# Clearing transfers placed behind the last weight load of a mixture kernel

## Chip, cores and metric

The kernel runs on one core of a Trainium2 chip. The metric is the device time of one execution in microseconds (us). The core has five engines with an instruction list each: TensorE (PE in the profile; PEld is its weight load), VectorE (DVE), ScalarE (ACT), GpSimd (POOL) and SyncE (SP). SP issues nearly all transfers here. Each engine goes through its list in order.

## What is computed

Three stages follow each other: attention with a window and a few sink positions, a gated MLP (called the first mixture here, `moe_`), and a routed mixture of eight experts (`moe2_`). Shapes: 2 x 8 heads x 768 positions x 64; then 1536 tokens of 512 values, an inner width of 1536, and eight experts with an inner width of 1024.

```python
scores = where(is_sink | in_window, q @ k.T / sqrt(D), -1e9)
x = softmax(scores) @ v                      # 1536 x 512 after the heads are joined
g = x @ w_gate                               # 512 x 1536
x = (g * sigmoid(g) * (x @ w_val)) @ w_out   # first mixture
do = x @ w_skip > 0                          # second mixture: only these tokens
e = argmax(x[do] @ gate); p = softmax(x[do] @ gate)[e]
out = x; out[do] += p * (relu(x[do] @ w1[e]) @ w2[e])
```

The arrays are float32, but the three weights of the first mixture arrive as 64-bit floats.

## The kernel before

The 1536 tokens are twelve blocks of 128. The first mixture runs in three phases of four blocks each (`PHASES`); a phase goes through twelve chunks of the inner width, and for each chunk PE makes the gate and value products (`proj`, L551) and, one chunk later, adds to the four output accumulators (`down`, L563). Attention of the next blocks is interleaved with that: while phase 0 works on blocks 0 to 3, PE also does blocks 4 to 7.

The weights of the first mixture come in 36 pieces of 512 KB (`load_w`, L154): gate, value and output for each of the twelve chunks. Since they are 64-bit, a piece lands in one of three staging buffers (`st`) and is converted to float32 by two steps on ACT (L169, L170) and two on DVE (L174, L175) in `convert`. The converted weights stay in fast memory for all phases, so the conversions may run well ahead of the chunk that needs them. `convert_w` converts one piece and starts the load of the piece three further on; `todo` holds the pieces whose load has not been traced yet. `prep` later splits a converted piece into a high and a low part (ring, L74 and L77) for PE.

For the experts, tokens are scattered into rows of a scratch tensor `xs` in DRAM, one region for each expert (L771, an indirect transfer issued on POOL). Rows that no token takes must hold zeros and a token number out of range, so the first 192 rows of each of the eight regions are written beforehand: `clear_rows` (L667) fills one tile `trash` with zeros on POOL and issues eight transfers of 387 KB from it on SP (L672), one at each `next(rows)` of the main loop. The main loop (L1373 to L1387) counts the steps `s` of phase 0, of which there are 37, three to a chunk; `clear_rows` starts at step 6, and the eight transfers are traced at the even steps from 14 to 28. `load_w` traces its last piece at step 29.

The order within an engine's list is set by a scheduler: it knows what each instruction depends on, and puts an instruction into its engine's list as soon as, by its own reckoning, the instruction could start and nothing traced earlier is ready. So work that is ready soon stands in the lists far ahead of the place where it was traced. `tc.issue_after(ins)` adds an edge of order: what is traced under it on the engine of `ins` comes behind `ins` in that engine's list, with no wait for `ins` to finish.

The q and k of the later blocks (from the ninth on) are loaded in 16 + 16 small pieces (`load_qk`, L109) and turned on DVE (`turned_a`, L322).

Of the kernel before, what the change touches and what calls it, by code (L numbers as in the profile page):

```python
# [10 lines left out]
I32 = mybir.dt.int32  # L11
# [4 lines left out]
P = 128  # L16

@with_exitstack
def build(ctx: ExitStack, tc: tile.TileContext, q, k, v, n_sink, window,
          wg, wv, wo, w_skip, w_gate, w1, w2, out):  # L20
    nc = tc.nc
# [30 lines left out]
    RW = DM + 4  # L52
    ES = NT + 2 * P
    HP = P // 2
# [75 lines left out]
        return rings[i // 4][:, i % 4, :]  # L130

    staged = []

    wsrc = {"g": wg, "v": wv, "o": wo}
    todo = [(nm, c) for c in range(NFC) for nm in "gvo"]

    def load_w():

        if not todo:
            return  # L140
        nm, c = todo.pop(0)
        src = wsrc[nm]
        t = wpc[nm, c // 4]
        if nm == "o":
            dst, s = t[:, c % 4, :], src[c * P:(c + 1) * P, :]
        else:
            dst = t[:, :, (c % 4) * P:(c % 4 + 1) * P]
            s = src[:, c * P:(c + 1) * P].rearrange("(a p) f -> p a f", p=P)
        if not wide:
            nc.sync.dma_start(out=dst, in_=s)  # L150
            return
        st = stp.tile([P, 512, 2], I32, tag="st", name="st")
        si = st if nm == "o" else st.rearrange("p (a f) t -> p a f t", a=KD)
        nc.sync.dma_start(out=si.rearrange("p f t -> p (f t)") if nm == "o" else si.rearrange("p a f t -> p a (f t)"), in_=s.bitcast(I32))  # L154
        staged.append((dst, si))

    def convert(dst, si):
# [21 lines left out]
    def convert_w():  # L179
        if staged:  # L180
            convert(*staged.pop(0))
        converted[0] += 1
        load_w()
# [438 lines left out]
    xs = dram.tile([NE * ES, RW], F32, name="xs")  # L622
# [11 lines left out]
    def make_trash(trash):  # L634
        nc.gpsimd.memset(trash, 0.0)
        nc.gpsimd.iota(trash.bitcast(I32)[:, DM + 1:DM + 2], pattern=[[0, 1]], base=NT, channel_multiplier=0)

    def make_routing_consts():
        with nc.allow_non_contiguous_dma(reason="small"):
            nc.sync.dma_start(out=wgs[:, :, 0:NE], in_=w_gate.rearrange("(a p) e -> p a e", p=P))  # L640
            nc.sync.dma_start(out=wgs[:, :, NE:NE + 1], in_=w_skip.rearrange("(a p o) -> p a o", p=P, o=1))
        nc.gpsimd.memset(ones, 1.0)
        act_copy(upper, ident[:, HP:P])
        nc.gpsimd.affine_select(out=before, in_=ones, compare_op=ALU.is_gt, fill=0.0, base=0, pattern=[[1, P]], channel_multiplier=-1)
        it = mo.tile([P, RW], F32, tag="x2", name="it", bufs=4)[:, 0:P].bitcast(I32)
        nc.gpsimd.iota(it, pattern=[[1, P]], base=0, channel_multiplier=0)
        nc.gpsimd.tensor_copy(slot, it)
        first_block = tc.issue_after(begun["DVE"])
        first_block.__enter__()

        nc.vector.tensor_scalar(out=code, in0=slot[:, 0:NE + 1], scalar1=float(NE), scalar2=-1.0, op0=ALU.subtract, op1=ALU.mult)

        nc.vector.tensor_scalar(out=first, in0=slot[:, 0:NE + 1], scalar1=float(ES // P), scalar2=None, op0=ALU.mult)
        nc.gpsimd.memset(first[:, NE:NE + 1], float(4 * NE * ES // P))
        nc.gpsimd.iota(tokid, pattern=[[P, NT // P]], base=0, channel_multiplier=1)
        nc.vector.tensor_copy(seen, first)
        first_block.__exit__(None, None, None)

    def turn_gates():
        t = attp.tile([P, KD, P], F32, tag="att", name="wgT")  # L660
        for kk in range(KD):
            nc.tensor.transpose(out=t[0:NE + 1, kk], in_=wgs[:, kk, :], identity=ident)
        c = mo.tile([P, RW], F32, tag="x2", name="wgc", bufs=4)[0:NE + 1, 0:DM]
        act_copy(c, t[0:NE + 1].rearrange("p a f -> p (a f)"))
        nc.sync.dma_start(out=wgt, in_=c)

    def clear_rows():  # L667

        trash = mo.tile([P, RW], F32, tag="x2", name="trash", bufs=4)
        make_trash(trash)  # L670
        for e in range(NE):
            nc.sync.dma_start(out=xs[e * ES:e * ES + P + HP, :].rearrange("(b p) c -> p b c", b=2),  # L672
                              in_=trash[0:(P + HP) // 2].unsqueeze(1).to_broadcast([(P + HP) // 2, 2, RW]))
            yield

    def route(pools, toks, rows, apart=None):
# [166 lines left out]
    def finish(g, tiles):  # L843
        take, turn, logits, close = routing(g, tiles)
        n = len(tiles)
        for i, t in enumerate(tiles):
            take(i, acc.pop((g, t)))
        for i in range(n):
            turn(i)
            if i > 0:  # L850
                logits(i - 1)
        logits(n - 1)
        close()
# [485 lines left out]
    load_v(0)  # L1339
    make_consts()  # L1340
    load_w()
    load_w()
    load_qk(1)
    load_w()
# [23 lines left out]
    for i, (g, t0, t1, c0, c1, want) in enumerate(PHASES):  # L1368
        pieces = (want - done) * (3 * NPAIR + 2)
        slots = 3 * (c1 - c0) - 1  # L1370
        s = 0
        emitted = 0
        for _ in mlp(i):  # L1373
            s += 1
            while done < want and emitted < pieces * s / slots:
                done = next(at, NB_ALL)
                emitted += 1
            if i == 0 and s == 6:
                make_routing_consts()
                rows = clear_rows()  # L1380
            if i == 0 and s > 12 and s % 2 == 0:
                next(rows, None)
            if i == 0 and s == 24:
                turn_gates()
            while apart and units < min(units_all, (s - 3) * units_all // 22):
                next(apart)
                units += 1  # L1387
        while done < want:
            done = next(at, NB_ALL)
        if i == 0:  # L1390
            for _ in rows:
                pass
        if done == NB_ALL and late is None:
            early.close()
            late = fast.enter_context(tc.tile_pool(name="late", bufs=2))
        if apart:
            for _ in apart:
                pass
            apart = None
        if i in APART:  # L1400
            apart = finish_apart(g, range(t0, t1), late_rows if late else early_rows)
            next(apart)
            units, units_all = 0, (t1 - t0) * (NE + 1) + 1
        elif i + 1 == len(PHASES):
            with tc.manual_schedule(engines={mybir.EngineType.PE}):
                finish_last(g, range(t0, t1), late)
                experts(late)
        elif c1 == NFC:
            finish(g, range(t0, t1))
# [33 lines left out]
```

## Time and profile before

| | us |
|---|---|
| median of three runs | 608.57 |
| lowest and highest run | 607.16, 608.84 |
| the profiled execution, its own time | 606.38 |
| span of its profile | 604.7 |

| engine | busy us in the span |
|---|---|
| PE | 569.9 |
| DVE | 456.1 |
| ACT | 347.8 |
| POOL | 206.7 |

Times in the profile count from the start of the span. A wait names the instruction that released it as the profile infers it. In an order of time, the bracket at the end of a row is the idle time of that engine just before, and what ended it.

### The profile page before, as it was taken

The page shows a single profiled execution, that of the slowest core. Times are in us where ns is not written, and L with a number is a line of the kernel's source. Part 1 is how long each engine was busy: PE and PEld are TensorE (multiplying, and loading weights), DVE is VectorE, ACT ScalarE, POOL GpSimd, SP SyncE. Part 2 cuts the span into 40 slices and gives each one's busy share as a digit, 9 for nine tenths or more (in the row PEclk, how much of TensorE's full clock was granted, in tenths as well). Part 3 has the DMA queues.
Part 4 walks back from the last instruction along what each step waited for, and adds up shares of the span by engine and source line. Part 5 has one row for each costly group of instructions (what it writes and reads, how often), then busy time and mean ns, then how long its engine had stood idle before and what let it go on. Part 6 is the DMA issues. An engine that isn't in the chain of part 4 may idle for free. (4 is left out here: it accounts for less than half of the span.)

```text
span 604.7 us, 10096 instructions
## 1 busy us (share of the span) xinstructions
PE 569.9 (94%) x3049; PEld 440.3 (73%) x3049; DVE 456.1 (75%) x1170; ACT 347.8 (58%) x818; POOL 206.7 (34%) x291
## 2 busy tenths in 40 slices
PE   7999999799999999999999999999987999999992
PEld 4657767567777777777888888888875877777771
DVE  4798897897656899986564999854368897999930
ACT  4898786776555565655444453443146666766710
POOL 3474362566444241412320100030143334536310
PEclk7899999999999999999999999999997999999997
DMA  8866888653302422000002531300159777879401
GB/s 200 195 167 159 244 247 260 190 175 88 88 11 36 111 59 68 19 19 0 19 1 88 192 105 53 123 30 1 63 169 325 256 259 244 286 252 315 171 5 35
DMA packets 90597, 80.53 MB, mean 133 GB/s; under 512 B 53515, under 2 KB 65803, under 8 KB 90530
## 3 DMA queue, kind: packets, MB, share of 16 engines
q1 hardware_dynamic: 87730, 74.07, 40.9%
q0 software_dynamic: 2512, 5.68, 2.7%
q8 instruction: 29, 0.48, 0.3%
q14 instruction: 38, 0.31, 0.2%
q10 hardware_dynamic: 288, 0.00, 0.0%
HBM read 70.09 MB, written 12.00 MB: 136 GB/s over the span
## 5 line engine op out<-in xcount | busy, mean ns | idle before, releaser
L551 PE MATMUL gv<-xt,ring 128*128 128x512 f32 x864 | 216.9, 401 | 0.0
L551 PEld LDWEIGHTS gv<-xt,ring 128*128 128x128 f32 x864 | 158.1, 188 | 38.3 <-issue 2.0
L74 ACT ACTIVATE ring<-w 128x512 fp32r<-128x512 f32 x113 | 70.8, 629 | 94.9 <-PE gv L551 72.4
L77 DVE TENSOR_TENSOR w<-stage,w 128x512 fp32r<-128x512 f32 x96 | 85.2, 930 | 8.1 <-ACT w L74 6.3
L563 PE MATMUL acc<-ring,hh 128*128 128x512 f32 x256 | 82.5, 403 | 0.0
L74 ACT ACTIVATE w<-stage 128x512 fp32r<-128x512 f32 x128 | 71.5, 628 | 14.6 <-DMA stage<-in_moe_w_dram 10.5
L77 POOL TENSOR_TENSOR w<-stage,w 128x512 fp32r<-128x512 f32 x32 | 45.8, 1433 | 94.7 <-DVE ring L77 59.4
L77 DVE TENSOR_TENSOR ring<-w,ring 128x512 fp32r<-128x512 f32 x77 | 54.0, 701 | 26.7 <-ACT ring L74 26.7
L77 POOL TENSOR_TENSOR ring<-w,ring 128x512 fp32r<-128x512 f32 x36 | 48.7, 1354 | 51.1 <-ACT ring L74 46.7
L563 PEld LDWEIGHTS acc<-ring,hh 128*128 128x128 f32 x256 | 46.4, 188 | 11.8 <-issue 1.2
L718 DVE CUSTOM_DVE_ANT_0 wl<-x,wl 128x512 f32<-128x512 f32 x72 | 50.2, 697 | 1.1
L563 PE MATMUL acc<-ring,hl 128*128 128x512 f32 x128 | 50.9, 398 | 0.0
L364 ACT ACTIVATE p<-p,st 128x132 f32<-128x132 f32 x96 | 38.2, 400 | 17.2 <-DVE st L360 16.4
L1076 PE MATMUL yps<-w,hT 128*128 128x512 f32 x192 | 46.8, 398 | 0.8 <-ACTq L1115 0.5
L397 POOL TENSOR_SCALAR_AFFINE_SELECT pt<-pt 128x256 f32<-128x256 f32 x40 | 21.9, 548 | 73.6 <-ACT pt L74 73.6
L1050 PE MATMUL hps<-w,xh 128*128 128x512 f32 x128 | 42.8, 416 | 1.0
L1076 PEld LDWEIGHTS yps<-w,hT 128*128 128x128 f32 x192 | 35.4, 188 | 9.8 <-ACTq L1115 1.3
L344 PE MATMUL s<-kq 64*128 64x260 f32 (+1 forms) x144 | 34.9, 418 | 3.1 <-DVE st L360 1.1
L594 DVE TENSOR_TENSOR th<-th,gv 128x512 f32<-128x512 f32 x36 | 24.5, 681 | 14.4 <-PE gv L551 14.3
L771 POOL DMA_INDIRECT xs<-x,pi x12 | 12.1, 1012 | 60.2 <-issue 35.0
L175 DVE SCALAR_TENSOR_TENSOR w<-w,st 128x512 int32<-128x512 int32 x36 | 30.2, 839 | 2.3 <-ACT w L170 1.0
L344 PEld LDWEIGHTS s<-kq 64*128 64x128 f32 x144 | 16.9, 196 | 20.5 <-issue 10.5
(199 smaller groups left out, 958.7 us busy)
## 6 DMA issues: line engine op xcount, KB each, us to landing
stage<-in_moe_w_dram SPq DMA_DIRECT2D x128, 256.0 KB, 4.5
st<-in_moe_w_gate_dram SPq DMA_DIRECT2D x12, 512.0 KB, 4.9
st<-in_moe_w_val_dram SPq DMA_DIRECT2D x12, 512.0 KB, 4.9
st<-in_moe_w_out_dram SPq DMA_DIRECT2D x12, 512.0 KB, 5.6
xs<-trash SPq DMA_DIRECT2D x8, 387.0 KB, 5.6
vb<-in_v_dram SPq DMA_DIRECT2D x12, 256.0 KB, 4.6
out_dram<-x SPq DMA_DIRECT2D x12, 256.0 KB, 3.1
wl<-wgt SPq DMA_DIRECT2D x10, 256.0 KB, 4.1
```

Source lines behind the costliest of these rows:

```text
L74: nc.scalar.activation(out=out, in_=in_, func=ACTF.Copy, scale=scale)
L77: return (eng or nc.vector).tensor_tensor(out=out, in0=in_, in1=hi.bitcast(F32), op=ALU.subtract).ins
L175: nc.vector.scalar_tensor_tensor(out=di, in0=di, scalar=3, in1=low, op0=ALU.logical_shift_left, op1=ALU.bitwise_or)
L344: m_ = nc.tensor.matmul(out=ss[h][:, 0:nk], lhsT=x_, rhs=y_, start=m == 0, stop=m == len(terms) - 1)
L364: nc.scalar.activation(out=p[:, h], in_=p[:, h], func=ACTF.Exp, scale=-1.0, bias=st[:, h:h + 1], accum_out=su[:, h:h + 1])
L397: nc.gpsimd.affine_select(out=d[:, 0], in_=d[:, 1], compare_op=ALU.is_ge, fill=0.0, base=0, pattern=[[0, 2], [1, P]], channel_multiplier=-1)
L551: nc.tensor.matmul(out=ps, lhsT=w_[:, kk * P:(kk + 1) * P], rhs=x_[:, kk, t0 * P:t1 * P], start=kk == 0 and m == 0, stop=kk == KD - 1 and ...
L563: nc.tensor.matmul(out=acc[g, t], lhsT=h_[:, s], rhs=w_, start=c == 0 and m == 0, stop=c == last and m == 2)
L594: nc.vector.tensor_tensor(out=th, in0=th, in1=vp, op=ALU.mult)
L718: nc.vector.tensor_tensor_reduce(out=junk, in0=x2s[t][:, 0:DM], in1=row, scale=1.0, scalar=0.0, op0=ALU.mult, op1=ALU.add, accum_out=lp[:, ...
L1050: nc.tensor.matmul(out=ps[half], lhsT=x_[:, kk, :], rhs=w_[:, kk, :], start=kk == 0 and m == 0, stop=kk == KD - 1 and m == 2)
L1076: nc.tensor.matmul(out=y, lhsT=h_[:, c, :], rhs=w_[:, c % 4, :], start=c == 0 and m == 0, stop=c == NF2 - 1 and m == 2)
```

## The change

`load_w` keeps its last issue in `loaded`. The main loop calls for a clear only when no load is left to trace (`not todo`), which is from step 29 on, at each step instead of each second one; and each clear is put behind the last load in SP's list. What is cleared, and with what, stays the same.

```diff
     staged = []
+    loaded = []
...
         st = stp.tile([P, 512, 2], I32, tag="st", name="st")
         si = st if nm == "o" else st.rearrange("p (a f) t -> p a f t", a=KD)
-        nc.sync.dma_start(out=si.rearrange("p f t -> p (f t)") if nm == "o" else si.rearrange("p a f t -> p a (f t)"), in_=s.bitcast(I32))
+        d = nc.sync.dma_start(out=si.rearrange("p f t -> p (f t)") if nm == "o" else si.rearrange("p a f t -> p a (f t)"), in_=s.bitcast(I32))
+        loaded[:] = [d.ins]
         staged.append((dst, si))
...
         for e in range(NE):
-            nc.sync.dma_start(out=xs[e * ES:e * ES + P + HP, :].rearrange("(b p) c -> p b c", b=2),
-                              in_=trash[0:(P + HP) // 2].unsqueeze(1).to_broadcast([(P + HP) // 2, 2, RW]))
+            with tc.issue_after(loaded[0]):
+                nc.sync.dma_start(out=xs[e * ES:e * ES + P + HP, :].rearrange("(b p) c -> p b c", b=2),
+                                  in_=trash[0:(P + HP) // 2].unsqueeze(1).to_broadcast([(P + HP) // 2, 2, RW]))
             yield
...
-            if i == 0 and s > 12 and s % 2 == 0:
+            if i == 0 and s > 12 and not todo:
                 next(rows, None)
```

## Rows read from the trace of the kernel before

**Rows 1.** The page: busy us of each engine, share of the span, instructions.

```profile
PE 569.9 (94%) x3049; PEld 440.3 (73%) x3049; DVE 456.1 (75%) x1170; ACT 347.8 (58%) x818; POOL 206.7 (34%) x291
```

**Rows 2.** Stretches: start:end, length, busy PE PEld DVE ACT POOL, clock, DMA share, GB/s.

```profile
60.00:80.00 20.00, 20.00 (x109) 14.54 (x106) 16.43 (x41) 16.17 (x36) 7.37 (x8) 1.00 0.80 239
80.00:115.00 35.00, 29.25 (x156) 21.72 (x155) 30.01 (x66) 25.36 (x61) 16.20 (x19) 1.00 0.81 241
115.00:140.00 25.00, 23.76 (x140) 18.12 (x139) 23.32 (x54) 21.40 (x51) 14.66 (x20) 1.00 0.52 171
140.00:160.00 20.00, 19.96 (x97) 14.89 (x96) 13.50 (x37) 12.18 (x33) 13.48 (x17) 1.00 0.28 50
160.00:440.00 280.00, 279.07 (x1448) 221.82 (x1446) 206.61 (x592) 136.46 (x319) 62.88 (x111) 1.00 0.20 59
```

**Rows 3.** Waits of PE, 80 to 115 us: total, times, longest.

```profile
PE tpt L390 <- DVE st L360: 4.4, 2, 3.1
PE s L344 <- ACT pt L74: 1.1, 1, 1.1
```

**Rows 4.** Waits of ACT, 80 to 115 us.

```profile
ACT st L169 <- DMA st<-in_moe_w_gate_dram: 4.7, 3, 3.5
```

**Rows 5.** Order of time around the longest wait: start, duration, engine, line, operation.

```profile
104.85 0.66 ACT L169 ACTIVATE st<-st 128x512 int32<-128x512 uint16 x1 [3.46 <-DMA st<-in_moe_w_gate_dram]
...
105.54 0.69 DVE L174 SCALAR_TENSOR_TENSOR st<-st 128x512 int32<-128x512 int32 x1 [2.53 <-ACT st L169]
...
106.91 0.98 PE L344 MATMUL s<-kq 64*128 64x260 f32 x4 [1.07 <-ACT pt L74]
...
112.55 0.41 PE L390 MATMUL tpt<-ident,p 128*128 128x128 f32 x2 [3.06 <-DVE st L360]
```

**Rows 6.** The clears: their issues, their size and landing, and their stretch.

```profile
L672 SPq DMA_DIRECT2D xs<-trash x8: 418/497/934, 59.7 to 112.4; - x8
...
xs<-trash SPq DMA_DIRECT2D x8, 387.0 KB, 5.6
...
59.00:113.00 54.00, 48.25 (x266) 35.59 (x266) 46.21 (x106) 40.17 (x92) 23.28 (x28) 1.00 0.80 238
```

**Rows 7.** Order of time: loads issued on SP and the ACT steps that waited for them.

```profile
82.18 0.39 SPq L154 DMA_DIRECT2D st<-in_moe_w_gate_dram  x1
...
86.06 0.67 ACT L169 ACTIVATE st<-st 128x512 int32<-128x512 uint16 x1 [1.09 <-DMA st<-in_moe_w_gate_dram]
...
97.07 0.37 SPq L154 DMA_DIRECT2D st<-in_moe_w_gate_dram  x1
97.49 0.50 SPq L672 DMA_DIRECT2D xs<-trash  x1
...
129.00 0.37 SPq L154 DMA_DIRECT2D st<-in_moe_w_gate_dram  x1
...
134.27 0.68 ACT L169 ACTIVATE st<-st 128x512 int32<-128x512 uint16 x1 [1.16 <-DMA st<-in_moe_w_gate_dram]
```

**Rows 8.** Order of time on PE, the wait that ends at 86.66.

```profile
86.66 0.41 PE L390 MATMUL tpt<-ident,p 128*128 128x128 f32 x2 [1.32 <-DVE st L360]
```

**Rows 9.** Order of time on SP; last, the scatters' durations and first and last start.

```profile
103.50 2.63 SPq L101 DMA_DIRECT2D qk<-in_q_dram  x1
...
135.16 0.34 SPq L154 DMA_DIRECT2D st<-in_moe_w_out_dram  x1
...
142.21 7.46 SPq L109 DMA_DIRECT2D qk<-in_k_dram  x16
...
L771 POOL DMA_INDIRECT xs<-x,pi x12: 968/980/1202, 291.3 to 445.1; - x12
```

**Rows 10.** Order of time on DVE and PE, behind 154 us.

```profile
154.36 0.45 DVE L322 STREAM_TRANSPOSE qk<-qk 128x256 f32<-128x256 f32 x1 [0.63 <-DMA qk<-in_q_dram]
...
157.39 0.28 DVE L360 CUSTOM_DVE_ANT_0 p<-s,mask 128x132 f32<-128x132 f32 x1
...
160.70 0.38 PE L390 MATMUL tpt<-ident,p 128*128 128x128 f32 x2
...
189.15 0.39 PE L344 MATMUL s<-kq 64*128 64x260 f32 x2
```

More of the change, by code (lines that the diff above doesn't have):

```diff
@@ L149, in load_w @@
         if not wide:
-            nc.sync.dma_start(out=dst, in_=s)
+            loaded[:] = [nc.sync.dma_start(out=dst, in_=s).ins]
             return
```

## The prediction

> **What bounds the kernel now.** I read the page's busy shares first: TensorE (PE) is busy 94% of the span [rows 1], so the time can only fall where PE is idle. The table of stretches then says where that is [rows 2]: nothing in 60 to 80 us, 35.00 - 29.25 = 5.75 us in 80 to 115, 25.00 - 23.76 = 1.24 us in 115 to 140, 0.04 us in 140 to 160, and 0.93 us in the whole 280 us after that. The transfers that the change moves are issued from 59.7 to 112.4 us [rows 6], so what they can give back is the idle of 60 to 140 us, 5.75 + 1.24 = 6.99 us, and no more.
>
> Then who ends those idle times. PE waits for VectorE (DVE) twice, 4.4 us, and for ScalarE (ACT) once, 1.1 us [rows 3]. Nothing there names a transfer. But ACT itself waits 4.7 us for the gate's weights, 3.5 us of it at once [rows 4]. The order of time joins the two [rows 5]: ACT stands 3.46 us until a gate load lands and converts it at 104.85; DVE, which takes the converted words, has then stood 2.53 us; and since each engine works through one fixed list, what stands behind the conversion is late too: the copy of a transposed block on ACT (PE idle 1.07 us until 106.91) and a mask step on DVE (PE idle 3.06 us until 112.55). These two are 1.07 + 3.06 = 4.13 of the 5.75 us.
>
> **Part 1, the eight clears leave 59 to 113 us.** What they take there: eight of 387 KB, 3.17 MB, of the 54 us x 238 GB/s = 12.9 MB that moved in this stretch with the sixteen engines 0.80 busy [rows 6]. At that rate one clear is 396 kB / 238 GB/s = 1.7 us and all eight are 13.3 us of the stretch (an estimate by the mean rate). What does a load gain? I compare landings, from the issue on SP to the ACT step that waited for them [rows 5, 7]. With a clear directly behind it in the queue (97.49): 97.07 to 104.85, 7.8 us. With none behind it: 82.18 to 86.06, 3.9 us; 129.00 to 134.27, 5.3 us. So the late load would land after 3.9 to 5.3 us, at 101.0 to 102.4, where ACT came to it at 104.85 - 3.46 = 101.4. Its wait falls from 3.46 to between 0 and 1.0 us: 2.5 to 3.5 us come back on ACT, and about as much (2.53, the whole hole) on DVE, and on PE behind them. I take 3.0, the middle, as the ends are close; 4.13 - 3.0 = 1.1 us of the two stalls stays, for DVE's list is full: in the next stretch, where no clear is issued, it is busy 23.32 of 25.00 us and PE still loses 1.24 us [rows 2].
>
> The other late load next to it, at 86.06 after 1.09 us, I cost at nothing: PE's 1.32 us before 86.66 end on a mask step of DVE [rows 8], an engine that has no wait for a conversion there. Bounds for part 1: 2.5 us by the first reading; by rates, if 80 to 115 becomes like 115 to 140 (1.24 / 25 = 0.05 idle per us), 5.75 - 35 x 0.05 = 4.0 us; and at most 6.99 us, all idle. Below nothing is possible too, see the rivals.
>
> **Part 2, they arrive behind the last load.** That load is issued at 135.16 [rows 9]. The new edge is one of order on SP alone: no semaphore is added and no other engine's list gets a wait. SP is then idle until the block's next q and k pieces at 142.21 (apart from two v loads), and DMA is busy 0.28 in 140 to 160 us [rows 2]. Eight issues of 0.50 us (the median of the eight) [rows 6] are 4.0 us of SP; eight transfers of 1.7 us are 13.3 us of the queue. Behind them are v of a later block, the 16 + 16 small pieces of k and q of the ninth block, later the gates' rows and the first mixture's output rows. Nobody but the scatter into the cleared rows waits for the clears themselves, and the first scatter is at 291.3, over 100 us on [rows 9]. PE makes the ninth block's first scores at 189.15, DVE turns its first piece at 154.36 [rows 10]: 35 us of cover for PE. I cost part 2 at nothing; should the scheduler put the clears later still, up to the end of the first mixture's steps, the sum is the same. The buffer that holds the zeros is given back later, but of its four slots the next are wanted by the gates' copy and then by the first mixture's output rows, both after the clears. If the cover is gone, part 2 is rival B's price.
>
> **Part 3, the list changes.** The queue's order is made by a scheduler that hoists loads and conversions ahead. With eight transfers fewer in the way it may place conversions earlier on ACT and DVE. The trace can't show this; both ends are from rows: gain up to the 6.99 us of idle; loss, if DVE's list grows as tight as in 80 to 115 (5.75 / 35 = 0.16 idle per us) in the 45 us on either side as well, 45 x 0.16 - 1.24 = 6 us. I take nothing, since the two full stretches without and with clears (115 to 140, 60 to 80) lose little, and keep both ends in the range with small weight.
>
> **Sum.** -3.0 + 0 + 0 = -3.0 us. The profiled execution took 606.38 us (span 604.7, 1.7 around it), 2.19 us under the median of 608.57; against itself 603.4, against the median **605.6 us**. After 160 us PE has 0.93 us of idle up to 440, so nothing there eats the gain; the experts' stage behind it starts on PE's and the routing's results, so it moves along.
>
> **Rival A: the queue had room, and DVE is the bound.** 0.80 busy leaves a fifth of the stretch; a load without a clear still came late (1.16 us at 134.27) [rows 7]; DVE is busy 30.01 of 35.00 us [rows 2]. A load is issued only when DVE has emptied one of three staging buffers, so loads that land sooner are only converted sooner, DVE's list is full in the same places, and the 3.06 us come back at another mask step. Against it: the 2.53 us in which DVE had nothing. It would keep 0 to 1.5 us of the 3.0: about 608 us. The Trainium skill, "DMA: Bandwidth & Descriptors", Specifications, gives about 358 GB/s as what one core gets from memory; by that the 12.9 MB would be 36 of the 54 us, the clears could have run in the gaps, and the sum would be near nothing, 608.6 us. The rows speak against the rule in so far as the queues moved 238 GB/s with their engines 0.80 busy [rows 6], which at full share would be 298.
>
> **Rival B, the slower side: the clears hold up the ninth block's q and k.** SP issues in order, and an issue can stand: the q load of 103.50 held SP for 2.63 us with much in flight [rows 9]. If eight clears in a row fill the queue, SP is done with them not at 139.5 but at 135.2 + 13.3 = 148.5, 6.3 us after the 142.21 of the first k piece. The q pieces follow by 7.5 us as before, so DVE's turns, which already wait for q (0.63 us before 154.36) [rows 10], would stand up to 6.3 us in the middle of DVE's list, and the mask step of 157.39 with them. PE has 160.70 - 157.39 = 3.3 us until the product that needs it, so about 3.0 us fall on PE. On top of rival A that is 611.6 us; with the forecast's gain kept the two cancel, 608.6. It decides if SP still issues clears after 142.2 plus the 3.3 us.
>
> **That it doesn't do what it says** is hardly open: the clears are traced when no load is left, with an edge behind the last one, so they can't run before it.
>
> **Chances.** Forecast, gain of 1.8 us or more: 0.55. Rival A, or gain and loss cancelling: 0.28. Rival B, or a list that became worse (part 3): 0.17. A measurement of this kernel can tell about 0.3%, 1.8 us, from no change; so faster 0.55, same 0.28, slower 0.17. The range: low end 602.6, the gain of 6.0 us that would leave 1 of the 7 us idle, under which I put 0.06; high end 610.2, within which rival A and the cheaper half of B lie; 0.13 above it. The forecast's own range is 604.0 to 606.7.
>
> **What would show it.** In the profile after: no clear before the last load; the 3.46 us wait of ACT for a gate load gone or under 1 us; PE's idle in 80 to 115 us from 5.75 to about 2.7; the last load issued earlier than 135.16 by about 3; the part after 160 us the same length. Part 2 is wrong if SP issues pieces of k later than 7 us after the last load, or DVE's turns stand over 1 us each. The prediction fails if PE's idle in 60 to 160 stays near 7 us with other names on it (rival A or part 3).

## The result and the profile after

The changed kernel takes 611.02 us (median of 15 runs, 609.49 to 616.28) against 607.16 us (604.17 to 611.42) of the kernel before, run beside it on the same chip: ratio 1.0068, with an interval of 1.0047 to 1.0090. It is slower, where the forecast was 605.6 us with a range of 602.6 to 610.2. The forecast was reckoned from the three runs known then, with a median of 608.57 us. The profiled execution took 609.74 us, its span is 608.0 us.

Line numbers after are one to three higher (the load is L155, the mask step L362, the clears L675). The stretches of the changed kernel, with the columns of [rows 2]:

```profile
60.00:80.00 20.00, 20.00 (x98) 14.40 (x95) 17.48 (x44) 17.37 (x40) 7.52 (x8) 1.00 0.73 211
80.00:115.00 35.00, 29.75 (x152) 21.90 (x151) 31.51 (x68) 26.58 (x61) 16.82 (x18) 0.95 0.75 219
115.00:140.00 25.00, 23.66 (x129) 17.78 (x130) 20.75 (x50) 19.28 (x46) 16.16 (x21) 0.93 0.30 91
```

PE is idle for 5.25 us in 80 to 115 us and 1.34 us in 115 to 140, 6.59 us together, where it was 6.99 us. So nothing came back, and two more things differ: VectorE (DVE) is busier in 80 to 115 us (31.51 us for 30.01), and the granted clock, 1.00 in all these stretches before, is 0.95 and 0.93. The waits in 80 to 115 us, first PE's, then that of ScalarE (ACT) for loads, answer [rows 3, 4]:

```profile
PE tpt L392 <- DVE st L362: 3.6, 2, 2.1
PE tqk L303 <- DVE xt L77: 1.7, 1, 1.7
...
ACT st L171 <- DMA st<-in_moe_w_val_dram: 3.1, 3, 1.6
```

The single wait of 3.46 us for a gate load is gone, as forecast. Other waits, all on DVE, stand in its place. Next SyncE (SP) in order of time, the answer to [rows 9]:

```profile
126.58 0.34 SPq L155 DMA_DIRECT2D st<-in_moe_w_out_dram  x1
...
143.77 7.46 SPq L109 DMA_DIRECT2D qk<-in_k_dram  x16
151.28 8.27 SPq L109 DMA_DIRECT2D qk<-in_q_dram  x16
...
161.62 8.79 SPq L675 DMA_DIRECT2D xs<-trash  x8
```

The last load is issued at 126.58 us instead of 135.16, 8.6 us earlier, and the eight clears come in one piece at 161.62, behind the ninth block's k and q. Nobody waits for them: PE has no idle in 140 to 200 us.

**A ruler.** To compare kernels whose clocks and starts differ, I use work that is the same in all of them. PE makes the attention output of a block in a run of small products (xps, L443 before, L445 after). Four of these runs serve as marks: A at 59.19 us in the profile of before, B at 97.67, C at 136.59 and D, the last, at 315.72. In after they start at 58.32, 96.57, 138.40 and 317.44. Between two marks PE has the same products to make (182 in B to C; a row can show one or two more or fewer). "Idle" between marks is the length less PE's busy time. The expectations below call B the second and C the third (at other places the ninth) pair's output step; "from the first gate product" means from 63.67 us of before. From A to B both kernels take 38.3 to 38.5 us. The rows from B to C and from C to D, first of before, then of after:

```profile
97.67:136.59 38.92, 33.55 (x182) 25.36 (x182) 33.30 (x71) 28.96 (x68) 20.02 (x26) 1.00 0.64 195
...
136.59:315.72 179.13, 178.92 (x1000) 139.04 (x999) 135.44 (x429) 100.92 (x263) 67.54 (x113) 1.00 0.18 43
```

```profile
96.57:138.40 41.83, 36.74 (x182) 27.35 (x181) 35.28 (x81) 31.38 (x74) 21.67 (x26) 0.92 0.57 165
...
138.40:317.44 179.04, 178.86 (x1000) 138.97 (x999) 130.62 (x420) 97.32 (x256) 65.90 (x114) 1.00 0.24 59
```

This is the result in four lines. The loss between A and D lies between B and C, 41.83 - 38.92 = 2.9 us. (Outside the marks, A comes 0.9 us earlier and the part behind D is 1.6 us longer in this pair of profiles; in the second pair the part behind D is 0.5 us shorter, so these two are not taken for the change.) Between B and C DVE does 81 steps instead of 71 (35.28 us for 33.30) and ACT 74 instead of 68. Of DVE's ten, two belong to one more converted piece (13 for 12, some 2.2 us); the others are short mask and softmax steps. Behind C, DVE does 9 steps fewer (130.62 us for 135.44), five of them conversion steps, and PE takes 179 us all the same, since it is idle for only 0.2 us there. Work of DVE and ACT has been moved out of a stretch where it cost nothing into one where PE waits for it.

It is the scheduler that moved it. In ACT's list the first seven gate steps (tanh) of the first phase have 13, 14, 18, 22, 26, 30 and 35 conversions ahead of them before, and 13, 15, 19, 24, 29, 33 and 36 after. With eight transfers out of SP's list it places loads and conversions earlier. What that does to PE shows best at a wait that the kernel before does not have. In order of time on PE, ACT and DVE of after:

```profile
103.40 0.44 PE L303 MATMUL tqk<-ident,qk 128*128 128x128 f32 x2 [1.66 <-DVE xt L77]
...
101.36 0.66 ACT L171 ACTIVATE st<-st 128x512 int32<-128x512 uint16 x1 [1.55 <-DMA st<-in_moe_w_val_dram]
101.92 0.58 ACT L74 ACTIVATE xt<-xps 128x512 fp32r<-128x512 f32 x1
...
102.66 0.68 DVE L77 TENSOR_TENSOR xt<-xps,xt 128x512 fp32r<-128x512 f32 x1
```

PE stands for DVE's xt step, that step takes ACT's copy of the attention output, and that copy now stands in ACT's list behind 26 conversions instead of 24. The 26th waits 1.55 us for its load. So the copy starts 5.4 us behind B, where it started 3.1 us behind B before:

```profile
100.81 0.58 ACT L74 ACTIVATE xt<-xps 128x512 fp32r<-128x512 f32 x1
```

In both profiles of before and in e5 and e8, which have ACT's old list, it is 3.1 us; in both profiles of after it is 5.3 to 5.4 us, and PE's wait is 1.66 and 1.63 us; in e6, which has the new lists and early clears, it is 6.1 us. The longest wait of after comes seven microseconds on, in order of time on DVE and then on PE:

```profile
105.06 1.58 DVE L177 SCALAR_TENSOR_TENSOR w<-w,st 128x512 int32<-128x512 int32 x1
...
107.37 0.89 DVE L176 SCALAR_TENSOR_TENSOR st<-st 128x512 int32<-128x512 int32 x1
108.36 1.58 DVE L177 SCALAR_TENSOR_TENSOR w<-w,st 128x512 int32<-128x512 int32 x1
109.87 0.48 DVE L351 COPY_PREDICATED s<-above,s 128x128 f32<-128x128 int32 x2
110.27 0.28 DVE L362 CUSTOM_DVE_ANT_0 p<-s,mask 128x132 f32<-128x132 f32 x1
...
106.55 0.71 PE L346 MATMUL s<-kq 64*128 64x260 f32 x4
107.19 1.42 PE L553 MATMUL gv<-xt,ring 128*128 128x512 f32 x5
110.70 0.57 PE L392 MATMUL tpt<-ident,p 128*128 128x128 f32 x2 [2.10 <-DVE st L362]
```

The scores (s) are done by 107.3 us, but DVE first goes through a conversion (107.37 and 108.36, 2.5 us) and only then comes to the masks of 109.87 and 110.27 that PE stands for. This order is not new: in the kernel before, the conversion of 109.22 and 110.22 us stands in front of the mask of 112.11, and PE waits 3.06 us there. So the longest wait of both kernels is DVE's conversion in front of a mask, and what the new lists add is the wait at 103.40. In idle time alone the two do not differ much between B and C (5.09 us in both profiles of after, 5.37 and 3.76 in those of before); PE's busy time is 3.2 us longer, at the lower clock, which is taken up under e7.

### The profile page after: what moved, and what is told of

Same layout as the page of the kernel before. It is cut to its first block, busy times and chain, and to the rows that moved or that the text cites. A ratio compares the mean times of both kernels' runs of the same rounds, so it can differ in the third digit from the quotient of the medians.

```text
span 608.0 us, 10101 instructions
## 1 busy us (share of the span) xinstructions
PE 573.4 (94%) x3049; PEld 442.4 (73%) x3049; DVE 456.0 (75%) x1170; ACT 348.2 (57%) x818; POOL 205.1 (34%) x291
## 5 line engine op out<-in xcount | busy, mean ns | idle before, releaser
L553 PE MATMUL gv<-xt,ring 128*128 128x512 f32 x864 | 220.0, 405 | 0.0
L553 PEld LDWEIGHTS gv<-xt,ring 128*128 128x128 f32 x864 | 160.1, 191 | 39.1 <-issue 2.0
L77 DVE TENSOR_TENSOR w<-stage,w 128x512 fp32r<-128x512 f32 x96 | 86.9, 946 | 7.5 <-ACT w L74 5.7
L366 ACT ACTIVATE p<-p,st 128x132 f32<-128x132 f32 x96 | 38.3, 401 | 16.8 <-DVE st L362 16.0
L1053 PEld LDWEIGHTS hps<-w,xh 128*128 128x128 f32 x128 | 23.9, 197 | 8.0 <-issue 3.1
```

The lines of the kernel that those rows point to most:

```text
L77: return (eng or nc.vector).tensor_tensor(out=out, in0=in_, in1=hi.bitcast(F32), op=ALU.subtract).ins
L366: nc.scalar.activation(out=p[:, h], in_=p[:, h], func=ACTF.Exp, scale=-1.0, bias=st[:, h:h + 1], accum_out=su[:, h:h + 1])
L553: nc.tensor.matmul(out=ps, lhsT=w_[:, kk * P:(kk + 1) * P], rhs=x_[:, kk, t0 * P:t1 * P], start=kk == 0 and m == 0, stop=kk == KD - 1 and ...
L1053: nc.tensor.matmul(out=ps[half], lhsT=x_[:, kk, :], rhs=w_[:, kk, :], start=kk == 0 and m == 0, stop=kk == KD - 1 and m == 2)
```

## The experiments

Two theories were put against each other. **Lists**: the moved transfers gain something, and the changed lists of PE, DVE and ACT lose more. **Transfers**: eight clears late and in one piece cost time by themselves. A third question came up on the way, whether the low clock is the loss.

Marks of all profiles, in us, from the rows in which each run of xps starts (A to B is 37.3 to 38.7 except where named):

| kernel | clears | lists of PE, DVE, ACT | B to C | C to D | A to D |
|---|---|---|---|---|---|
| before, its two profiles | early | old | 38.92, 37.27 | 179.13, 179.18 | 256.53, 255.11 |
| after, its two profiles | late | new | 41.83, 41.85 | 179.04, 179.04 | 259.12, 259.15 |
| e3, e9 (conversions held to the old counts) | late | near the old | 36.53, 38.17 | 179.32, 179.03 | 253.18, 254.54 |
| e4 (three for each gate step) | late | others | 34.59 | 183.57 | 256.45 |
| e5 | late | old, SP's new | 37.01 | 184.77 | 260.18 |
| e6 (A to B 42.67) | early | new | 43.17 | 179.04 | 264.88 |
| e7 (25 products added) | late | new | 40.84 | 179.02 | 258.15 |
| e8 | late | old, SP's too | 37.38 | 179.26 | 255.07 |
| e10 (four DVE steps added, B to C) | early | old | 46.01 | 178.94 | 263.09 |
| e11 (four DVE steps added behind C) | early | old | 39.12 | 178.91 | 256.69 |
| e12 (held a little more) | late | others | 36.94 | 182.69 | 256.94 |

### The two kernels again

No edit. The kernel before:

> The kernel before, unchanged, for a second trace and for the granted clock of each of its runs. All theories expect a ratio of 1.000 +- 0.003. If the clock is what makes the changed kernel slow, the mean granted clock here is higher than the 0.967 to 0.982 (mean 0.977) of the changed kernel's runs, by about 0.003 to 0.005. PE idle in 80 to 140 us about 7.0 us again, with the same releasers.

Measured: ratio 1.0007 (0.9970 to 1.0045). The mean granted clock of its runs is 0.979, against 0.977 for those of the changed kernel in the first comparison and 0.980 in the second, so the clock of whole runs does not tell the two kernels apart. The changed kernel:

> The changed kernel, unchanged, for a second trace. All theories expect a ratio of 1.005 to 1.009. Theory L (the conversions stand denser in ACT's and DVE's lists) expects PE to stand at the same instructions as in the first trace of it. If the low clock of 110 to 114 and 128 to 131 us is an accident, it stands elsewhere or not at all in this trace, and the time is 3 us shorter than that of a trace with it.

Measured: 609.17 us, ratio 1.0035 (1.0004 to 1.0065), a smaller loss than the first time and than expected, but still one. The marks of after agree within 0.03 us in A to D; those of before differ by 1.4 us, and by 1.65 us in B to C. There the second profile of before has idle times of PE of 1.73 us (before 113.25) and not 3.06 us. The row from B to C of this second profile of before:

```profile
101.11:138.38 37.27, 33.51 (x184) 25.11 (x183) 33.26 (x71) 29.12 (x68) 20.61 (x26) 1.00 0.71 215
```

PE's idle in 80 to 140 us is 5.58 us in it, not the 7.0 us expected, and the 1.07 us before the scores [rows 5] is not there. The gate load from which the forecast took its gain, again with a clear directly behind it in SP's list, is issued at 100.53 us in this profile. In order of time on ACT and DVE:

```profile
106.16 0.68 ACT L169 ACTIVATE st<-st 128x512 int32<-128x512 uint16 x1 [1.33 <-DMA st<-in_moe_w_gate_dram]
...
106.87 0.69 DVE L174 SCALAR_TENSOR_TENSOR st<-st 128x512 int32<-128x512 int32 x1 [0.41 <-ACT st L169]
```

It landed after 5.6 us and not after 7.8; ACT waited 1.33 us for it and not 3.46, DVE 0.41 us and not 2.53, with the clears where they had always been. So the 4.13 us of two stalls on which the forecast built were the size of one execution, not of the kernel.

### Late clears with the old pace of conversions (e3, e9), and with an even pace (e4)

The changed kernel, with each conversion held in ACT's list behind the gate step that it followed in the kernel before:

```diff
+    def hold(k):
+        got = [c for c, n in enumerate((13, 14, 18, 22, 26, 30, 35)) if n <= k]
+        return got[-1] if got and k < 36 else None
...
+            c_ = hold(converted[0])
+            if c_ is not None:
+                es.enter_context(tc.issue_after(tanhs[c_]))
             nc.scalar.activation(out=low, in_=h16[x + (1,)], ...
```

> The change, with the conversions on ACT held by order edges to the places that they had before (13, 14, 18, 22, 26, 30, 35 conversions ahead of the first seven tanh steps, against 13, 15, 19, 24, 29, 33, 36 in the changed kernel); the clears stay behind the last load. Theory L expects the loss gone: ratio 0.993 to 1.000, 603 to 607 us. The rival, that the clears at their new place (or the loads without them) cost the time whatever the lists, expects 1.005 to 1.009 as the change.

> The kernel with late clears whose conversions may not run ahead of the chunks by more than in the kernel before, timed a second time. Theory 'lists': as in its first profile, PE idle in 80 to 140 us about 3.6 us, nothing in 140 to 300 us, ratio 0.993 to 0.999. Rival (its gain was chance): ratio 1.000 or more, or PE idle of 6 us and more in 80 to 140.

Measured: 604.93 us, ratio 0.9982 (0.9948 to 1.0016), and the second time 606.48 us, 0.9977 (0.9948 to 1.0005). The clears stand as late as in after, and the loss is gone. PE's idle in 80 to 140 us is 3.63 us in the first profile and 4.94 us in the second, where 3.6 was expected. From A to B both take 37.3 us, 1.1 us less than before and than e8 below; only ACT's conversions are held here, so the other lists are near the old ones and not the same. The row from B to C in the first:

```profile
96.26:132.79 36.53, 33.41 (x182) 25.08 (x181) 33.09 (x73) 29.65 (x70) 20.97 (x26) 1.00 0.63 184
```

With an even pace, three conversions for each gate step:

```diff
+    def hold(k):
+        return (k - 13) // 3 if 13 <= k < 36 else None
```

> The change, with the conversions thinned out: three for each chunk (13, 15, 19, 22, 25, 28, 31, 34 ahead of the tanh steps) instead of up to five. Theory L expects PE's idle time in 80 to 140 us to fall below the 6.6 us of the change, to 3 to 5 us, and the ratio to 0.992 to 0.998. The rival (list density is not it) expects 1.004 to 1.009.

Measured: 610.01 us, ratio 1.0037 (1.0004 to 1.0070), near what the rival expected, though not for its reason. B to C is the shortest of all (34.59 us with 65 DVE steps), but behind C a new wait appears, and C to D takes 4.4 us more (2.0 us of them are busy time of PE, at a mean clock of 0.99). In order of time on PE:

```profile
145.69 0.33 PE L353 MATMUL s<-kq 64*128 64x132 f32 x1 [2.00 <-DVE kq L77]
```

Held back too far, the conversions cost time behind C instead, where PE waits for a step of DVE.

### The clears alone moved (e5, e8), the lists alone changed (e6)

Here the lists of whole engines are held: each step gets an edge of order behind the step that it followed in the list of one of the two kernels.

```diff
+    def follow(order, extra):
...
+        for e, ks in order.items():
+            xs_ = [clears[-1 - k] if k < 0 else traced[e][k] for k in ks]
+            for a, b in zip(xs_, xs_[1:]):
+                tc.add_manual_dep(b, a.name, mybir.DependencyInfo(mybir.DependencyClass.NoSync, mybir.DependencyReason.DATA), reason="order")
...
+            follow(ORDER, ())
```

e5 is the changed kernel with PE, DVE and ACT in the order of before; e6 is the kernel before with these three in the order of after, so that its clears stay among the loads. In both runs the lists of SP and POOL are left to the scheduler.

> The clears late, but TensorE, VectorE and ScalarE go through exactly the lists of the kernel before (each step held behind the one it followed there). Theory 'lists' (the loss comes from the changed lists, the moved transfers themselves gain what was forecast): from the first gate product to the ninth pair's output step (xps x32) 68.5 to 70 us instead of 72.4, PE idle in 80 to 115 us about 2.4 us, granted clock 1.00 in 60 to 160, ratio to the kernel before 0.993 to 0.999. Rival 'transfers' (eight clears in a row behind the last load cost time of their own): PE idle appears in 140 to 200 us, ratio 1.002 or more.

> The clears stay early, among the loads, as in the kernel before, but TensorE, VectorE and ScalarE go through exactly the lists of the changed kernel. Theory 'lists': the loss is all here, and the early clears add to it: the stretch from the first gate product to the ninth pair's output step takes 75 us or more (72.4 in the kernel before, 75.1 in the changed one), with granted clock 0.50 somewhere in 100 to 135 us, ratio 1.003 to 1.010. Rival 'transfers': these lists are as good as the old ones, 71 to 72.5 us, ratio 0.998 to 1.002.

Measured for e6: 616.46 us, ratio 1.0186 (1.0139 to 1.0232), more than expected. The new lists cost more with early clears than with late ones, 264.88 us from A to D against 259.12; ACT waits for loads in 80 to 115 us for 6.2 us, 3.2 and 3.0 us in two waits each. Under these lists, which need their loads sooner, the move is so worth 5.8 us; a part of that can be SP's own list, which the scheduler ordered a little differently here (a few q, k and weight loads stand earlier or later than in either kernel). The row from B to C of e6:

```profile
101.64:144.81 43.17, 35.19 (x183) 26.25 (x182) 35.38 (x79) 30.41 (x73) 21.85 (x26) 0.96 0.55 167
```

Measured for e5: 611.01 us, ratio 1.0103 (1.0062 to 1.0144), against what the theory of the lists expected. B to C is short (37.01 us), but a wait of 3.42 us stands behind it, at the place where no kernel had one. In order of time on PE, DVE and SP of e5:

```profile
211.31 2.93 PE L559 MATMUL gv<-xt,ring 128*128 128x512 f32 x6 [3.42 <-DVE th L601]
...
206.68 0.45 DVE L330 STREAM_TRANSPOSE qk<-qk 128x256 f32<-128x256 f32 x1 [4.33 <-DMA qk<-in_q_dram]
...
200.19 0.90 SPq L115 DMA_DIRECT2D qk<-in_q_dram  x2
...
201.68 1.51 SPq L707 DMA_DIRECT2D out_dram<-x  x3
203.24 1.19 SPq L115 DMA_DIRECT2D qk<-in_q_dram  x2
```

and the same place on SP in the kernel before:

```profile
201.16 2.57 SPq L109 DMA_DIRECT2D qk<-in_q_dram  x4
...
204.32 1.53 SPq L698 DMA_DIRECT2D out_dram<-x  x3
```

In e5 SP's list was left to the scheduler, and it puts the third and fourth q piece of a later block behind three output rows. DVE, held to the old order, turns that block's first piece early and stands 4.33 us for it. The clears had been issued 40 us before (156.89). To tell whether this is the clears or the mixture of lists, e8 holds SP's list too, with the eight clears cut out and put behind the last load and the ninth block's pieces (negative numbers are the clears):

```diff
-ORDER = {"PE": [...], "DVE": [...], "Activation": [...]}
+ORDER = {"PE": [...], "DVE": [...], "Activation": [...], "SP": [..., -1, -2, -3, -4, -5, -6, -7, -8, ...]}
```

> As the run in which the clears alone were moved, but SyncE too goes through the list of the kernel before, with the eight clears cut out and put behind the last load and the ninth block's pieces; so TensorE, VectorE, ScalarE and SyncE have the old lists and only the clears have another place. Theory 'lists': now the forecast's gain shows and nothing takes it back: PE idle in 80 to 140 us at most 4.5 us (7.0 before), none over 0.5 us in 140 to 300, ratio to the kernel before 0.992 to 0.999. Rival 'transfers' (late clears delay something behind them whatever the lists): the PE wait of 3.4 us near 211 us is there again, ratio 1.003 or more.

Measured: 605.06 us, ratio 0.9975 (0.9946 to 1.0004). The wait at 211 us is gone (PE is idle for 0.35 us in 200 to 300 us), so it came from the mixture. PE's idle in 80 to 140 us is 4.04 us, within the 4.5 expected, although the clock fell here too (0.93 in the second row):

```profile
80.00:115.00 35.00, 32.73 (x173) 24.30 (x172) 32.12 (x74) 28.62 (x67) 19.36 (x21) 1.00 0.68 205
115.00:140.00 25.00, 23.23 (x130) 17.39 (x129) 22.84 (x52) 19.99 (x48) 12.94 (x19) 0.93 0.47 150
...
200.00:300.00 100.00, 99.65 (x584) 77.83 (x583) 85.27 (x287) 56.44 (x147) 32.42 (x56) 1.00 0.17 44
```

So the clears, moved alone, gain about what e3 and e9 gain by the runs, and PE has no wait behind 140 us that comes of them (0.35 us of idle in 140 to 300). Transfers as the cause of the loss is ruled out. By the marks the gain of e8 is small: from A to D it takes 255.07 us, as much as the second profile of before (255.11) and 1.5 us less than the first. PE's idle between B and C is 2.45 us in it, for 5.37 and 3.76 before, but its busy time is 34.93 us for 33.5, at the lower clock, so that 1.4 us of what the idle gave back was lost again.

### Is it the clock? (e7)

In after the granted clock falls to 0.50, which is 1.2 GHz, twice:

```profile
110.90:114.00 3.10, 3.10 (x9) 2.38 (x8) 2.09 (x6) 1.25 (x6) 1.02 (x2) 0.50 0.71 216
127.90:131.00 3.10, 3.10 (x9) 2.38 (x8) 2.56 (x7) 1.83 (x7) 0.88 (x2) 0.50 0.57 182
```

both right behind a wait of PE for DVE (2.10 us before 110.70, 0.81 us before 127.42), and in its second profile at the same places (behind 2.06 and 0.80 us). PE's busy time from B to C for the same 182 products is 36.74 - 33.55 = 3.2 us longer, as much as the whole loss. e7 keeps the lists of after on PE, DVE and ACT and puts 25 products that add zero into these two waits:

```diff
+                if t0 == 0 and g == 0 and kk * 3 + m == FILL.get((nm, c), (0, 0))[0] - 1:
+                    for _ in range(FILL[nm, c][1]):
+                        f_ = nc.tensor.matmul(out=ps[:, 0:256], lhsT=nought, rhs=idle[0:HP, 0:256], start=False, stop=False)
```

> The changed kernel with its lists held as they are, and 25 small products that add zero put into two of PE's waits (18 in the wait of 2.1 us that ends at 110.7, 7 in the wait of 0.8 us that ends at 127.4). Theory 'clock' (these waits make the granted clock fall to 0.50 at 111 and 128 us, and that is the 3.4 us): the clock stays at 1.00 there, the stretch from the first gate product to the ninth pair's output step falls from 75.1 to about 71.7 us, ratio to the kernel before 0.998 to 1.002. Rival (the clock falls whatever PE does in these waits, or the loss is not the clock): two spells at 0.50 stay, 75 to 76 us, ratio 1.003 to 1.008.

Measured: 610.98 us, ratio 1.0079 (1.0043 to 1.0114). The clock stays at 1.00 from 60 to 160 us, so the waits were what it fell behind. But the time hardly moves; from the first gate product it is 74.2 us to the ninth pair's output step, for 75.1 before the products were added, so neither expectation came out. From B to C, and on PE:

```profile
97.40:138.24 40.84, 36.52 (x207) 27.31 (x206) 36.27 (x80) 30.43 (x73) 21.55 (x26) 1.00 0.57 169
...
109.42 2.13 PE L569 MATMUL gv<-ident 64*128 64x256 bf16 x18
112.23 0.41 PE L403 MATMUL tpt<-ident,p 128*128 128x128 f32 x2 [0.68 <-DVE st L373]
...
121.11 0.41 PE L403 MATMUL tpt<-ident,p 128*128 128x128 f32 x2 [1.61 <-DVE st L373]
```

40.84 us instead of 41.83: one of the 2.9 us came back. The products ran faster, and PE then stood 1.61 us instead of 0.21 at the next mask step. One thing hides a part of the gain: the first of these masks comes on DVE 14.4 us behind B (111.80) and not 13.7 (110.27), since DVE had stood and worked longer in front of it, before the added products had any say. From that mask to C it is 26.4 us instead of 28.1. So keeping the clock up is worth 1.0 to 1.7 us here. The Trainium skill, "TensorE: Matmul & The Clock Gate", Terms, puts the cost of a lower clock at the time spent at it times the missing share, which by the two rows above would be 6.2 x 0.5 = 3.1 us (an estimate); the measured 1.0 to 1.7 us decide. Where PE waits for another engine, about half or more of what the clock took would have been waiting time.

### More of DVE's work, early and late (e10, e11)

The kernel before with its lists held, and four conversion steps done twice (the second gives the same words): 2.9 us more of DVE between B and C.

```diff
             nc.vector.scalar_tensor_tensor(out=low, in0=high, scalar=-0x80000000, in1=low, op0=ALU.bitwise_and, op1=ALU.bitwise_or)
+            if converted[0] in (25, 27, 29, 31):
+                extra.add(nc.vector.scalar_tensor_tensor(out=low, in0=high, ...).ins.name)
```

> The kernel before with all its lists held, and four of VectorE's conversion steps (the 26th, 28th, 30th and 32nd piece's first step, 0.72 us each, which give the same words when done twice) done twice: 2.9 us more of VectorE's work in 97 to 137 us, nothing else. Theory 'VectorE's list sets the length of this stretch': the stretch from the second to the third pair's output step, 37.3 to 38.9 us in the kernel before and 41.8 in the changed one, becomes 40 to 42 us, ratio 1.003 to 1.008. Rival (VectorE has 5.6 us of idle there that takes the steps in): 37 to 39 us, ratio 0.998 to 1.002.

Measured: 613.46 us, ratio 1.0104 (1.0068 to 1.0140).

```profile
96.68:142.69 46.01, 37.75 (x183) 28.37 (x182) 37.62 (x74) 29.35 (x68) 21.36 (x26) 0.89 0.56 168
...
111.68 0.66 PE L401 MATMUL tpt<-ident,p 128*128 128x128 f32 x2 [3.66 <-DVE st L371]
...
129.96 0.69 PE L401 MATMUL tpt<-ident,p 128*128 128x128 f32 x2 [2.61 <-DVE st L371]
```

B to C became 7.1 to 8.7 us longer (46.01 against 38.92 and 37.27), more than twice the work added and more than expected. PE's idle is 8.3 us instead of 5.4 and 3.8, and the clock 0.89. DVE's busy time rose by more than the four steps, by 4.3 us (37.62 for 33.30): the four take 2.9 us, and the twelve second conversion steps now take 14.4 us for 11.2, as more of them take over 1.5 us (see the end of this document). The 5.6 us in which DVE is idle there took nothing in. The control puts the same amount behind C:

```diff
                     nc.vector.scalar_tensor_tensor(out=lo, in0=h, scalar=0.5, in1=hi.bitcast(F32), op0=ALU.mult, op1=ALU.subtract)
+                    for _ in range(2 if ph == 0 and c in (7, 8) else 0):
+                        extra.add(nc.vector.scalar_tensor_tensor(out=lo, in0=h, ...).ins.name)
```

> The control to the run with four conversion steps done twice: the kernel before with all its lists held, and 3 us more of VectorE's work (the split of the eighth and ninth chunk's result, 0.7 to 0.9 us, done three times instead of once), but at 155 to 168 us, where VectorE is busy 0.6 of the time and PE always. Theory 'VectorE's list sets the length of the stretch before 140 us, and there alone': from the third pair's output step to the last one PE has no new idle, ratio to the kernel before 0.997 to 1.003. Rival (any 3 us of VectorE's work lengthen the kernel): 1.004 to 1.012 as in the earlier stretch.

Measured: 607.56 us, ratio 1.0020 (0.9991 to 1.0049), and from C to D:

```profile
139.78:318.69 178.91, 178.73 (x1000) 139.06 (x999) 137.22 (x433) 100.97 (x263) 67.95 (x112) 1.00 0.17 41
```

Four steps more (433 for 429; the four take 2.8 us) and no time more (178.91 for 179.13).

### Held back a little more (e12)

```diff
-        got = [c for c, n in enumerate((13, 14, 18, 22, 26, 30, 35)) if n <= k]
+        got = [c for c, n in enumerate((13, 14, 18, 22, 25, 29, 33)) if n <= k]
```

> Late clears, and conversions held back a little more than in the kernel before: 25, 29 and 33 instead of 26, 30 and 35 ahead of the fifth, sixth and seventh chunk's gate step. Theory 'VectorE's list': a step or two less in the stretch from the second to the third pair's output step makes it 35 to 36.5 us (36.5 and 38.2 in the run with 26, 30 and 35), without a new wait behind 140 us; ratio 0.991 to 0.998. Rival: the conversions come too late and PE waits for one behind 140 us, as in the run with three for each chunk; ratio 0.999 to 1.004.

Measured: 609.51 us, ratio 1.0045 (1.0012 to 1.0078). It came out at the slow end of what the rival expected, and the rival's reason was right: B to C is 36.94 us, no shorter than with the old counts, and behind C PE waits again:

```profile
143.24 0.44 PE L311 MATMUL tqk<-ident,qk 128*128 128x128 f32 x2 [1.72 <-ACT pt L74]
147.83 0.33 PE L354 MATMUL s<-kq 64*128 64x132 f32 x1 [1.12 <-DVE kq L77]
```

The old counts lie between two losses: more ahead of time is paid before C, less behind it.

**Better than both?** e3, e8 and e9 keep the late clears and the old pace. They are 0.5 to 0.9% under the two ratios of after; with 0.9975 to 0.9982 and intervals that reach 1 they can't be told from the kernel before by one of them alone. Taken together, against the runs of the kernel before beside them, the three give 0.9979 (0.9963 to 0.9995): a gain of about 1.3 us, just clear of noise.

## Why the prediction was wrong

**The step that failed is Part 3**, "I take nothing": the changed lists of the scheduler were costed at zero with both ends "in the range with small weight". They cost 4.1 to 4.8 us: from A to D, after takes 259.1 us, and with late clears it takes 255.1 us with the old lists (e8) and 253.2 and 254.5 with the old pace of conversions (e3, e9), on average 254.3. The reason given, that the stretches without and with clears lose little idle, looked at idle and not at what stands in the lists of ACT and DVE in front of the steps that PE waits for, nor at the clock that falls behind such waits. The loss end that the step did work out, 6 us, was near the size and of the right kind ("if DVE's list grows as tight"), though it was sought on either side of 80 to 115 us and came between 97 and 138.

**Part 1, the clears leave: about half the size at most, and from a stall that was one execution's.** The named wait of 3.46 us went, and with the old lists or pace PE's idle in 80 to 115 us fell to 2.27 us (e8), 2.37 (e3) and 2.91 (e9), where 2.7 was forecast. But in the second profile of before, with the clears still early, that wait is 1.33 us and the idle in 80 to 140 us is 5.58 us, not 6.99. From A to D the move is worth 255.8 - 254.3 = 1.5 us by the mean of before's two profiles against the mean of the three, and 0.7 us against e8 alone, the one run in which only the clears moved; the two profiles of before lie 1.4 us apart. By the runs it is about 1.3 us. So 3.0 was two to four times too much, and the error is that the size of a stall, and the landing of 7.8 us that it came from, were taken from one execution. Rival A said that 0 to 1.5 us of the 3.0 would be kept, since DVE's list is full; with the old lists that is what remained. Its first ground, that the queue had room, holds better than the prediction's answer to it: 298 GB/s was worked out there as the rate at full share, but single microseconds at a share of 1.00 move up to 393 GB/s (81 to 82 us of before).

**The sum** is then -0.7 + 4.1 with e8, or -1.5 + 4.8 with the mean of the three: +3.3 us, which is what the profiles of before and after differ by from A to D. The medians give +3.9 and, in the second comparison, +2.0 us. The split holds for the lists as they meet late clears; with early clears the new lists cost more (e6).

**Part 2, the clears behind the last load, cost nothing: right.** They were issued even later than the last load, at 161.62, and PE's idle in 140 to 200 us is nil. By its letter the prediction's own sign against Part 2 came (pieces of k 17 us behind the last load, not 7), but only since the last load went earlier: the k pieces start 5.4 us behind C, for 5.6 before, and no turn of DVE for that block stands for more than 0.44 us. Rival B's price was never paid in after, as the scheduler put the clears behind the q and k that it feared for. Its mechanism, a turn of q that DVE comes to before the pieces have landed, is real: it is e5's 3.42 us, set off by SP's order and not by the clears, as e8 shows.

**What was to show it.** No clear before the last load: right. The last load about 3 us earlier: it was 8.6, and the surplus was a sign of the changed lists. The same length behind 160 us: right (179.04 for 179.13 from C to D). The condition of failure, PE's idle in 60 to 160 us near 7 us with other names on it, is what came: 6.59 us in 80 to 140, 4.6 of it on the mask step and 1.7 on a step that was not in [rows 3].

**What stays open.** Why 2.9 us more of DVE in e10 became 7 to 8.7 us is accounted for (idle 2.9 to 4.5 us more, the rest at the lower clock) but not explained step by step. How the loss of after divides between waits and clock is known only in part: e7 says that half or more of the clock's part is not a cause of its own, and that was shown for the lists of after alone, in one profile. The edge on SP was not run without the later call. Built without the edge, the lists of all engines are instruction for instruction those of after, so the later place of the clears in the program is enough.

## What to carry to other kernels

Where a scheduler writes the lists, taking transfers out of one queue changes the lists of all engines: compare how much of each engine's work stands in each stretch before and after, and what stands in front of the steps that the busiest engine waits for, and cost a step by the stretch it lands in. Work of a second engine is free where PE is never idle (9 steps fewer, or 4 more, changed nothing behind C) and dear where PE waits for that engine's next step; its idle time there was no cover. If an edit is meant to move transfers alone, hold the order of the rest, and take the size of a stall from more than one execution.

## What the runs showed of the hardware

The granted clock fell to 0.50 behind some of PE's waits, long ones and short ones, and not behind others: it fell behind 3.66 us in e10 (before 111.68; 0.50 in 112 to 114 us), behind 2.10 and 0.81 us in after, 2.38 us in e11 (before 113.44; 0.50 in 114 to 116 us) and 0.77 us in e8 (before 126.36; 0.50 in 127 to 129 us), yet not behind the 3.06 us of [rows 5] or the 0.77 us at the same place in before (127.13). What decides between them is not shown here.

The second conversion step takes 0.68 us or more than twice as long. The two of 1.58 us shown above lie beside a GpSimd (POOL) step of the same size; in after, in order of time on POOL and DVE:

```profile
104.80 1.30 POOL L77 TENSOR_TENSOR ring<-w,ring 128x512 fp32r<-128x512 f32 x1 [5.23 <-ACT ring L74]
...
107.69 1.71 POOL L77 TENSOR_TENSOR ring<-w,ring 128x512 fp32r<-128x512 f32 x1
...
103.26 0.68 DVE L177 SCALAR_TENSOR_TENSOR w<-w,st 128x512 int32<-128x512 int32 x1
```

against the 1.58 us of the two at 105.06 and 108.36 above. The Trainium skill, "SBUF — State Buffer", Summary: rules for kernel authors, says that of a DVE step with two inputs in fast memory and a GpSimd step that reads it, the later one waits for the other to finish. This trace agrees: the two steps end at 106.64 and 109.94, each 0.54 us behind POOL's (106.10 and 109.40). A conversion that falls beside POOL's splits so holds DVE for 1.58 us. In the kernel before, the two at this place take 1.73 and 1.77 us, so this is not what the change brought; how much it weighs in front of a mask was not measured by itself.
